# Dealing every PSUM bank by hand instead of by pools, in a fused attention and gated-MLP kernel on one core

The chip is one Trainium2; the kernel runs on one of its cores. The metric is device time in microseconds (us) from launch to end. The profile's span, from the first to the last instruction, is some 1.7 us shorter.

## The reference

```python
x = A_x                                              # 1 x 2048 x 512, bf16
g = sigmoid((x * gate_w).sum(-1, keepdims=True))
# A: linear attention, 32 heads of 16
q, k, v = split(x @ wqkv)
phi_q = concat(softmax(q @ w_phi), softmax(-(q @ w_phi)))     # phi_k likewise
a = (phi_q @ (phi_k.T @ v)) / (phi_q . sum(phi_k) + 1e-6) @ wo
# B: gated MLP with a spatial product over the 2048 rows
z1, z2 = split(gelu(x @ w_in))                       # 688 columns each
b = (z1 * (w_sp @ layernorm(z2) + b_sp)) @ w_out
return g * a + (1 - g) * b
```

## The kernel before

A tile is 128 rows, so there are 16 of them. TensorE runs three stages. First come z2 and z1 of every tile (to about 46 us), then k, v and the accumulation of kv mixed with the first spatial tiles (to about 120 us). Last comes a loop that does, for each tile, one q projection, one spatial half (`gg`), one attention tile (`at`) and one output tile (`acc`). Before an output tile, DMA transposes bring the attention tile's result o and the spatial tile's result `ucat` into place as oT and uT. TensorE's results go to PSUM, of which the program uses eight banks; a bank is free again once ScalarE or VectorE has copied it out, which is called its eviction. Pools give the banks out: a pool hands the next tile a bank that its own plan, made while the kernel is built, sees free first. Below, "old hand-off" is the closing of the one pool and the opening of two others at the start of the last stage, "new hand-off" what the change puts in its place.

```python
def x_T(i):                       # transposes of x tile i, and their copies to SBUF
    parts = [(0, 1), (1, NDT)] if i == 0 else [(0, 2), (2, NDT)] if i == 1 else [(0, NDT)]
    for k, (d0, d1) in enumerate(parts):
        tp = psF.tile([P, NDT, P], BF16, name="tp", tag="pq", bufs=2)
        ...                       # k == 1: copied by ScalarE, else by VectorE

def gate_T():                     # the gate becomes column FH of w_z2, for the second column half
    gt = psF.tile([P, NDT], FP32, name="gt", tag="pq", bufs=2)
    nc.tensor.matmul(gt[:, :], lhsT=gaterow[:, :], rhs=ident[:, 0:NDT], start=True, stop=True)
    nc.vector.tensor_copy(out=w_z2[:, :, FH], in_=gt[:, :])

def ba_store(acc, tt, c0, c1, on_dve):
    ob = work.tile([P, c1 - c0], BF16, name=f"ob{c1 - c0}")       # work: two buffers
    ...
        nc.scalar.activation(out=ob[:, :], in_=acc, func=AF.Copy, scale=g_inv[:, tt:tt + 1])
        nc.scalar.dma_start(out=dst, in_=ob[:, :])

    # the last stage; the k, v stage had psK with six banks for everything
    w_main, w_rem, wo_t = load_out_weights()      # 1.9 MB on ScalarE's queue, issued at once
    psK_cm.__exit__(None, None, None)
    mm_pool = ...tile_pool(name="psG", bufs=2, ...)               # q and spatial tiles
    psC = ...tile_pool(name="psC", bufs=4, ...)                   # output tiles
    attn_tile(0)
    for i in range(NT - 1):
        if i + nq < NT:
            q_tile(i + nq)
        gg_next()
        attn_tile(i + 1)
        if i > 0:
            ba_step(i - 1)        # four outputs make a group; its evictions come together
```

The softmax here doesn't subtract the row's maximum and nothing guards it: scores larger than these inputs give would overflow.

Of the kernel before, what the change touches and what calls it, by code (L numbers as in the profile page):

```python
# [14 lines left out]
P = 128  # L15
# [20 lines left out]
def kernel(  # L36
# [90 lines left out]
    load_z2w(nc.sync, 2)  # L127
    nc.scalar.dma_start(out=gaterow[0:NDT, :], in_=gate_w.rearrange("(dt p) -> dt p", p=P))
    load_z2w(nc.scalar, 3)
    for i in range(2, 4):  # L130
        nc.sync.dma_start(out=xs[:, i, :], in_=x2[i * P:(i + 1) * P, :])
    for h in range(2):
        nc.sync.dma_start(
            out=w_z1[:, 2 * h:2 * h + 2, :], in_=w_in_v[:, 2 * h:2 * h + 2, 0:FH])
# [42 lines left out]
    for i, u in enumerate(ucat):  # L177
        nc.gpsimd.memset(u[:, FH:FPAD] if i % 2 == 0 else u[:, 0:FPAD - FH], 0.0)

    psA_cm = tc.tile_pool(name="psA", bufs=3, space=bass.MemoryType.PSUM, reuse_waits="tile")  # L180
    psA = psA_cm.__enter__()

    def zp_tile():
        return psA.tile([P, 2, CH], FP32, name="zp")

    def z_one(zp, tt, wt, w, dt, j):
        n = HF if j == 0 else w - HF
# [23 lines left out]

    def z2_first_two():
        zps = [zp_tile() for _ in range(2)]

        def one(tt, dt, j):
            z_one(zps[tt], tt, w_z2, FH + 1, dt, j)

        x_T(0)
        warm_up(3, P)
        one(0, 0, 0)  # L220
        x_T(1)
        one(0, 1, 0)
        warm_up(2, P)
        one(1, 0, 0)
        one(1, 1, 0)
        gate_T()
        one(0, 2, 0)
        one(1, 2, 0)
        for dt in range(2):
            one(0, dt, 1)  # L230
            one(1, dt, 1)
        x_T(2)
        one(0, 3, 0)
        one(1, 3, 0)
        one(0, 2, 1)
        one(0, 3, 1)
        z2_out(0, zps[0])
        x_T(3)
        one(1, 2, 1)
        one(1, 3, 1)  # L240
        z2_out(1, zps[1])

    def z1_tile(tt):
        zp = z_mm(tt, w_z1, FH)
# [15 lines left out]
                op0=ALU.subtract, op1=ALU.mult,  # L260
            )

    wp = zp_tile()

    def warm_up(n, w=CH):
        for _ in range(n):
            nc.tensor.matmul(  # L267
                wp[:, 0, 0:w], lhsT=nc.const_aps.tensor(1.0, [P, P], BF16),
                rhs=nc.const_aps.tensor(1.0, [P, w], BF16), start=True, stop=True)

    def x_T(i):
        parts = [(0, 1), (1, NDT)] if i == 0 else [(0, 2), (2, NDT)] if i == 1 else [(0, NDT)]
        for k, (d0, d1) in enumerate(parts):
            tp = psF.tile([P, NDT, P], BF16, name="tp", tag="pq", bufs=2)
            for dt in range(d0, d1):
                nc.tensor.transpose(tp[:, dt, :], xs[:, i, dt * P:(dt + 1) * P], ident[:, :])  # L276
            dst = xT[:, d0:d1, i * P:(i + 1) * P]
            if k == 1:
                nc.scalar.copy(out=dst, in_=tp[:, d0:d1, :])
            else:  # L280
                with tc.high_priority():
                    nc.vector.tensor_copy(out=dst, in_=tp[:, d0:d1, :])

    def gate_T():
        gt = psF.tile([P, NDT], FP32, name="gt", tag="pq", bufs=2)
        nc.tensor.matmul(gt[:, :], lhsT=gaterow[:, :], rhs=ident[:, 0:NDT], start=True, stop=True)
        nc.vector.tensor_copy(out=w_z2[:, :, FH], in_=gt[:, :])

    def b_T():
        bt = psF.tile([P, NT], FP32, name="bt", tag="pq", bufs=2)  # L290
        nc.tensor.matmul(bt[:, :], lhsT=brow[:, :], rhs=ident[:, 0:NT], start=True, stop=True)
        nc.vector.tensor_copy(out=bT[:, :], in_=bt[:, :])

    def wphi_fold():
        wps = psF.tile([P, NDT, P], FP32, name="wps", tag="pq", bufs=2)
        for kc in range(NDT):
            nc.tensor.matmul(
                wps[:, kc, :], lhsT=eexp[:, :],
                rhs=wphiE[:, kc * 8:(kc + 1) * 8, :].rearrange("e h f -> e (h f)"),
                start=True, stop=True,  # L300
            )
        nc.vector.tensor_tensor(
            out=wphi[:, :, :], in0=wps[:, :, :],
            in1=mask_bd[:, None, :].to_broadcast([P, NDT, P]), op=ALU.mult,
        )

    def fold(qk, dt):
        dst = wq_p if qk == 0 else wk_p
        fps = psF.tile([P, CH], FP32, name="fps", tag="pq", bufs=2)
        for kc in range(NDT):  # L310
            nc.tensor.matmul(  # L311
                fps[:, kc * P:(kc + 1) * P],
                lhsT=wqkT[:, qk * 4 + kc, dt * P:(dt + 1) * P],
                rhs=wphi[:, kc, :],
                start=True, stop=True,
            )
        if dt % 2 == 1:
            nc.scalar.copy(out=dst[:, dt, :], in_=fps[:, :])
        else:
            nc.vector.tensor_copy(out=dst[:, dt, :], in_=fps[:, :])  # L320

    with tc.manual_schedule(engines={mybir.EngineType.PE, mybir.EngineType.Activation}):
        warm_up(6)
        warm_up(4, P)
        z2_first_two()
        z2_tile(2)
        z2_tile(3)
        b_T()
        for c in range(NCH):
            ts = list(range(c * 4, c * 4 + 4))  # L330
            for tt in ts:
                if c > 0:
                    z2_tile(tt)
                if c >= 2 and tt % 2 == 0:
                    fold(3 - c, (tt % 4) // 2)
            for tt in ts:
                z1_tile(tt)
                if c >= 2 and tt % 2 == 0:
                    fold(3 - c, 2 + (tt % 4) // 2)
            z2_norm(ts)  # L340
            if c == 1:
                wphi_fold()
# [3 lines left out]
    early_cm.__exit__(None, None, None)  # L346
    psM = ctx.enter_context(
        tc.tile_pool(name="psM", bufs=1, space=bass.MemoryType.PSUM, reuse_waits="tile"))
    psK_cm = tc.tile_pool(name="psK", bufs=6, space=bass.MemoryType.PSUM, reuse_waits="tile")
    mm_pool = psK_cm.__enter__()  # L350
    work = ctx.enter_context(tc.tile_pool(name="work", bufs=2, reuse_waits="tile"))
    kvp_cm = tc.tile_pool(name="kvp", bufs=2, side="right", reuse_waits="tile")
    kvp = kvp_cm.__enter__()

    def mm_tile():
        return mm_pool.tile([P, CH], FP32, name="mm")

    def expo(pool, name, bufs, tt, w):
        ps = mm_tile()
        for dt in range(NDT):  # L360
            nc.tensor.matmul(ps[:, :], lhsT=xT[:, dt, tt * P:(tt + 1) * P], rhs=w[:, dt, :],  # L361
                             start=(dt == 0), stop=(dt == NDT - 1))
        e = pool.tile([P, H, 2, DH], BF16, name=name, bufs=bufs)
        for a in range(2):
            nc.scalar.activation(  # L365
                out=e[:, :, a, :], in_=ps[:, :].rearrange("p (h f) -> p h f", f=DH),
                func=AF.Exp, scale=1.0 - 2.0 * a)
        z = work.tile([P, H, 2], FP32, name="zs")
        nc.vector.tensor_reduce(  # L369
            out=z[:].rearrange("p h a -> p (h a)"), in_=e[:].rearrange("p h a f -> p (h a) f"),  # L370
            axis=AX.X, op=ALU.add,
        )
        return e, z
# [6 lines left out]
            in1=ratio[:, :, None].to_broadcast([P, H, DH]), op=ALU.mult)  # L380

    def k_tile(tt):
        ek, z = expo(kvp, "ek", 5, tt, wk_p)
        rk = kvp.tile([P, H, 2], FP32, name="rk", bufs=3)
        nc.vector.reciprocal(out=rk[:], in_=z[:])
        even_out(ek, z, rk[:, :, 1])
        return ek, rk

    def q_tile(tt):
        eq, z = expo(work, "eq", 3, tt, wq_p)  # L390
        rq = work.tile([P, H], FP32, name="rq")
        nc.vector.reciprocal(out=rq[:], in_=z[:, :, 1])
        even_out(eq, z, rq[:])
        eqT = work.tile([P, 8, P], BF16, name="eqT", bufs=7)
        nc.sync.dma_start_transpose(out=eqT[:, :, :], in_=eq[:].rearrange("p h a f -> p (h a f)"))
        eqTs[tt] = eqT
# [49 lines left out]
        nc.scalar.dma_start(out=w_rem[P - REM:P, :], in_=B_w_out[0:REM, :])  # L446
        return w_main, w_rem, wo_t

    def gg_half(tt, j):
        gp = mm_tile()  # L450
        c0 = (tt % 2) * (FPAD - FH)
        for st in range(NT):
            nc.tensor.matmul(  # L453
# [53 lines left out]
            nc.scalar.dma_start(out=dst, in_=ob[:, :])  # L507

    def acc_tile():
        return psC.tile([P, CH], FP32, name="acc")  # L510

    def ba_tile(tt, cuts=(0, D)):
        for h, (c0, c1) in enumerate(zip(cuts, cuts[1:])):
# [20 lines left out]
    Q_AT = (5, 7, 9, 11, 13, 15)  # L534
    ggs = [(tt, j) for tt in range(NT) for j in range(2)]

    def gg_next():
        tt, j = ggs.pop(0)
        gg_half(tt, j)
        if j == 1:  # L540
            uTs[tt] = u_T(tt)

    with tc.manual_schedule(engines={mybir.EngineType.PE, mybir.EngineType.Activation}):
# [3 lines left out]
        for tt in range(NT):  # L547
# [3 lines left out]
            pend.append((tt, ek, v_tile(tt, rk)))  # L551
            if len(pend) == 3:
                kv_acc(*pend.pop(0))
            gg_next()
            if tt in Q_AT:
                q_tile(Q_AT.index(tt))
        nc.scalar.activation(out=g_el[:, :], in_=glog[:, :], func=AF.Exp)
        nc.vector.tensor_scalar(out=g_1p[:, :], in0=g_el[:, :], scalar1=1.0, scalar2=None, op0=ALU.add)
        nc.vector.reciprocal(out=g_inv[:, :], in_=g_1p[:, :])
        for p_ in pend:  # L560
# [3 lines left out]
        kvw_cm.__exit__(None, None, None)  # L564
        outw = ctx.enter_context(
            tc.tile_pool(name="outw", bufs=1, side="right", reuse_waits="tile"))
        gg_next()
        w_main, w_rem, wo_t = load_out_weights()
        nq = len(Q_AT)
        psK_cm.__exit__(None, None, None)  # L570
        mm_pool = ctx.enter_context(
            tc.tile_pool(name="psG", bufs=2, space=bass.MemoryType.PSUM, reuse_waits="tile"))
        psC = ctx.enter_context(
            tc.tile_pool(name="psC", bufs=4, space=bass.MemoryType.PSUM, reuse_waits="tile"))
        attn_tile(0)
        for i in range(NT - 1):
            if i + nq < NT:
                q_tile(i + nq)
            gg_next()
            attn_tile(i + 1)  # L580
            if i > 0:
                ba_step(i - 1)
# [32 lines left out]
```

## Time and profile before

| | |
|---|---|
| time, median of 3 | 210.49 us (210.31 to 210.69) |
| span of the profiled execution | 208.8 us |
| TensorE | 203.5 us busy, 97% |
| waits of TensorE on another engine or a DMA | q on ucat, twice, 1.0 us in all; transposes on a copy, 0.4 us |

TensorE is the bound, so time is won or lost only where it stands still. The list of waits counts from the modelled end of a matmul and therefore understates a wait. The distances between starts of matmuls do not. Line numbers differ between the kernels: q is L361 before and L369 after, the spatial tile L453 and L460, its eviction (`ucat`) L458 and L465, the exponentials of q L365 and L373.

### The profile page before, as it was taken

The numbers are of one execution on the slowest core, as the hardware profiler recorded it, in microseconds if no ns is written. First come the engines' busy times: TensorE is split into PE (matmuls) and PEld (weight loads), VectorE is DVE, ScalarE is ACT, GpSimd is POOL, SyncE is SP. The second block draws the span as 40 slices with busy tenths as digits, with TensorE's granted clock in tenths as the row PEclk, the third lists the DMA queues.
The fourth block names the chain that finished last, engine by engine and source line by source line (L and its number), as shares of the span: only waits on it lengthen the run. The fifth ranks groups of instructions, "written<-read, shape, count | busy, mean of one in ns | idle before, by whom it ended". The sixth has DMA issues, their size and how long they took to land.

```text
span 208.8 us, 3779 instructions
## 1 busy us (share of the span) xinstructions
PE 203.5 (97%) x1455; PEld 122.2 (59%) x1455; DVE 132.0 (63%) x282; ACT 75.4 (36%) x122; POOL 46.5 (22%) x78
## 2 busy tenths in 40 slices
PE   8999999999999999999999989999999999999994
PEld 4666676665566555656565655555455555565642
DVE  2477786865977776979797676755538563353330
ACT  3666666666322233332323032222251223301322
POOL 7020202020532315334242430422204220010000
PEclk9999999999999999999999999999999999999999
DMA  6998999999932012240422299493562659355542
GB/s 196 230 174 154 250 285 211 290 259 219 290 76 42 0 38 52 41 84 16 81 48 40 50 227 305 84 146 73 105 164 54 115 101 143 75 101 78 129 111 75
DMA packets 88986, 27.20 MB, mean 130 GB/s; under 512 B 82984, under 2 KB 88968, under 8 KB 88968
## 3 DMA queue, kind: packets, MB, share of 16 engines
q1 hardware_dynamic: 84224, 22.43, 56.7%
q10 hardware_dynamic: 4712, 4.53, 7.3%
q8 instruction: 11, 0.18, 0.4%
q14 instruction: 7, 0.06, 0.1%
q0 software_dynamic: 32, 0.00, 0.0%
HBM read 4.41 MB, written 2.10 MB: 31 GB/s over the span
## 4 chain that ended last, share of the span: by engine, by line
PE 93%; ACT 2%; DVE 2%; DMA 1%; ACTq 0%; issue 0%
PE mm L453 34%; PE zp L188 18%; PE mm L361 13%; PE acc L492 8%; PE mm L401 7%; PE acc L490 6%; PE kvacc L417 2%; PE zp L267 2%; PE at L466 2%; DMA out_dram<-ob 1%; PE acc L495 1%; ACT ob L506 1%; PE fps L311 1%; ACT eq L365 1%; PE tp L276 1%; DVE zs L369 1%
## 5 line engine op out<-in xcount | busy, mean ns | idle before, releaser
L453 PE MATMUL mm<-z2all,wspT 128*128 128x344 bf16 x512 | 79.9, 309 | 0.1
L453 PEld LDWEIGHTS <-wspT 128*128 128x128 bf16 x512 | 49.0, 98 | 26.0 <-issue 0.9
L188 PE MATMUL zp<-w_z,xT 128*128 128x344 bf16 (+1 forms) x256 | 40.1, 310 | 0.0
L365 ACT ACTIVATE eq<-mm 128x512 bf16<-128x512 f32 x32 | 17.4, 594 | 51.7 <-PE mm L361 31.0
L369 DVE TENSOR_REDUCE zs<-eq 128x64 f32<-128x1024 bf16 x16 | 19.5, 1219 | 21.7 <-ACT eq L365 21.6
L458 DVE SCALAR_TENSOR_TENSOR ucat<-mm,bT,z1all 128x344 bf16<-128x344 f32 x32 | 17.6, 550 | 21.6 <-PE mm L453 21.6
L188 PEld LDWEIGHTS <-xT 128*128 128x128 bf16 x256 | 24.5, 98 | 11.1 <-issue 0.2
L378 POOL TENSOR_TENSOR eq<-eq,ratio 128x512 bf16<-128x512 bf16 x16 | 16.9, 1058 | 51.1 <-DVE ratio L377 40.2
L365 ACT ACTIVATE ek<-mm 128x512 bf16<-128x512 f32 x32 | 17.3, 600 | 27.1 <-PE mm L361 27.1
L506 ACT ACTIVATE ob<-acc,g_inv 128x512 bf16<-128x512 f32 (+1 forms) x16 | 10.9, 680 | 33.9 <-PE acc L495 23.4
L369 DVE TENSOR_REDUCE zs<-ek 128x64 f32<-128x1024 bf16 x16 | 19.3, 1208 | 2.8 <-ACT ek L365 2.8
L361 PEld LDWEIGHTS <-xT 128*128 128x128 bf16 x128 | 12.4, 98 | 13.9 <-issue 1.2
L492 PE MATMUL acc<-slabs,uT 128*128 128x512 bf16 (+2 forms) x85 | 20.1, 366 | 0.0
L378 POOL TENSOR_TENSOR ek<-ek,ratio 128x512 bf16<-128x512 bf16 x16 | 16.9, 1059 | 2.0 <-DVE ratio L377 1.2
L361 PE MATMUL mm<-wq_p,xT 128*128 128x512 bf16 x64 | 16.4, 379 | 1.0 <-DVE ucat L458 1.0
L490 PE MATMUL acc<-slabs,oT 128*128 128x512 bf16 (+2 forms) x68 | 16.6, 366 | 0.0
L401 PE MATMUL mm<-wv_sb,xT 128*128 128x512 bf16 x64 | 16.4, 379 | 0.0
L361 PE MATMUL mm<-wk_p,xT 128*128 128x512 bf16 x64 | 16.3, 379 | 0.0
L206 DVE BATCH_NORM_STATS2 bn<-z2all 128x6 f32<-128x344 bf16 x32 | 14.9, 503 | 0.0
L245 ACT ACTIVATE z1all<-zp 128x688 bf16<-128x688 f32 x16 | 11.9, 744 | 6.7 <-PE zp L188 6.7
L203 ACT ACTIVATE z2all<-zp 128x688 bf16<-128x688 f32 x16 | 11.8, 744 | 6.8 <-PE zp L188 6.3
L405 POOL CAST vr<-rk 128x32 bf16<-128x32 f32 x16 | 3.4, 212 | 45.7 <-PE mm L453 35.5
(77 smaller groups left out, 155.4 us busy)
## 6 DMA issues: line engine op xcount, KB each, us to landing
out_dram<-ob ACTq DMA_DIRECT2D x15, 128.0 KB, 2.2
slabs<-in_B_w_out_dram ACTq DMA_DIRECT2D x2, 640.0 KB, 6.2
w_z<-in_B_w_in_dram SPq DMA_DIRECT2D x2, 344.0 KB, 5.0
w_z<-in_B_w_in_dram ACTq DMA_DIRECT2D x3, 172.0 KB, 3.4
xs<-in_A_x_dram SPq DMA_DIRECT2D x4, 128.0 KB, 3.2
wv_sb<-in_A_wqkv_dram SPq DMA_DIRECT2D x1, 512.0 KB, 4.6
slabs<-in_A_wo_dram ACTq DMA_DIRECT2D x1, 512.0 KB
uT<-ucat SPq DMA_TRANSPOSE x16, 2.8
```

Of the source, the lines that this page charges most:

```text
L188: nc.tensor.matmul(zp[:, j, 0:n], lhsT=xT[:, dt, tt * P:(tt + 1) * P], rhs=wt[:, dt, j * HF:j * HF + n], start=(dt == 0), stop=(dt == NDT ...
L206: nc.vector.bn_stats(out=bn6[:, tt, j, :], in_=z2v[:, j, :])
L361: nc.tensor.matmul(ps[:, :], lhsT=xT[:, dt, tt * P:(tt + 1) * P], rhs=w[:, dt, :], start=(dt == 0), stop=(dt == NDT - 1))
L365: nc.scalar.activation(out=e[:, :, a, :], in_=ps[:, :].rearrange("p (h f) -> p h f", f=DH), func=AF.Exp, scale=1.0 - 2.0 * a)
L369: nc.vector.tensor_reduce(out=z[:].rearrange("p h a -> p (h a)"), in_=e[:].rearrange("p h a f -> p (h a) f"), axis=AX.X, op=ALU.add,)
L378: nc.gpsimd.tensor_tensor(out=e[:, :, 1, :], in0=e[:, :, 1, :], in1=ratio[:, :, None].to_broadcast([P, H, DH]), op=ALU.mult)
L401: nc.tensor.matmul(v_ps[:, :], lhsT=xT[:, dt, tt * P:(tt + 1) * P], rhs=wv_sb[:, dt, :], start=(dt == 0), stop=(dt == NDT - 1))
L453: nc.tensor.matmul(gp[:, 0:HF], lhsT=wspT[:, st, tt * P:(tt + 1) * P], rhs=z2all[:, st, j * HF:(j + 1) * HF], start=(st == 0), stop=(st == ...
L458: nc.vector.scalar_tensor_tensor(out=ucat[tt % NU][:, c0 + j * HF:c0 + (j + 1) * HF], in0=gp[:, 0:HF], scalar=bT[:, tt:tt + 1], in1=z1all[ ...
L490: nc.tensor.matmul(acc, lhsT=oT[:, g, :], rhs=wo_t[:, g, c0:c1], start=(g == 0), stop=False)
L492: nc.tensor.matmul(acc, lhsT=uT[:, i + ft, :], rhs=w_main[i][:, ft, c0:c1], start=False, stop=False)
L506: nc.scalar.activation(out=ob[:, :], in_=acc, func=AF.Copy, scale=g_inv[:, tt:tt + 1])
```

## The change

It is meant to take away TensorE's three waits. Each half of x tile 1 is to get its own bank, the six banks of the k, v stage are to go on in the last stage in order of age, and one load is to replace two.

```diff
-    for i in range(2, 4):
-        nc.sync.dma_start(out=xs[:, i, :], in_=x2[i * P:(i + 1) * P, :])
+    nc.sync.dma_start(
+        out=xs[:, 2:4, :], in_=x2[2 * P:4 * P, :].rearrange("(i p) d -> p i d", p=P))
 ... # in z2_first_two:
+        tp1 = psA.tile([P, 2, 2 * CH], BF16, name="tp1", tag=next_turn("zp", 3))
-        x_T(1)
+        for h in range(2):
+            x_T(1, 2 * h, 2 * h + 2,
+                tp1[:, h, 0:2 * P].rearrange("p (d n) -> p d n", n=P), on_act=h == 1)
 ...
         gate_T()
-        one(0, 2, 0)
-        one(1, 2, 0)
         for dt in range(2):
             one(0, dt, 1)
             one(1, dt, 1)
+        one(0, 2, 0)
+        one(1, 2, 0)
 ... # in the last stage:
-        psK_cm.__exit__(None, None, None)
-        mm_pool = ...psG, bufs=2
-        psC = ...psC, bufs=4
+        q_bank, g_bank, *acc_banks = [next_turn("mm", 6) for _ in range(6)]
 ...
-                q_tile(i + nq)
-            gg_next()
+                q_tile(i + nq, bank_tile(q_bank))
+            gg_next(bank_tile(g_bank))
```

More of the change, by code (lines that the diff above doesn't have):

```diff
@@ L178, with next_turn, pq_tile @@
         nc.gpsimd.memset(u[:, FH:FPAD] if i % 2 == 0 else u[:, 0:FPAD - FH], 0.0)
-    psA_cm = tc.tile_pool(name="psA", bufs=3, space=bass.MemoryType.PSUM, reuse_waits="tile")
+    psA_cm = tc.tile_pool(name="psA", bufs=1, space=bass.MemoryType.PSUM, reuse_waits="tile")
     psA = psA_cm.__enter__()
+    turn = {"zp": 0, "pq": 0, "mm": 4}
+    def next_turn(kind, n):
+        turn[kind] += 1
+        return f"{kind}{(turn[kind] - 1) % n}"
     def zp_tile():
-        return psA.tile([P, 2, CH], FP32, name="zp")
+        return psA.tile([P, 2, CH], FP32, name="zp", tag=next_turn("zp", 3))
+    def pq_tile(shape, dtype=FP32):
+        return psF.tile(shape, dtype, name="pq", tag=next_turn("pq", 2))
     def z_one(zp, tt, wt, w, dt, j):
@@ L213, in z2_first_two, with warm_up @@
         zps = [zp_tile() for _ in range(2)]
+        tp1 = psA.tile([P, 2, 2 * CH], BF16, name="tp1", tag=next_turn("zp", 3))
+        turn["zp"] -= 1
+        def warm_up(n, w=CH):
+            for _ in range(n):
+                nc.tensor.matmul(
+                    zps[0][:, 1, 0:w], lhsT=nc.const_aps.tensor(1.0, [P, P], BF16),
+                    rhs=nc.const_aps.tensor(1.0, [P, w], BF16), start=True, stop=True)
         def one(tt, dt, j):
             z_one(zps[tt], tt, w_z2, FH + 1, dt, j)
-        x_T(0)
+        warm_up(6)
+        warm_up(5, P)
+        x_T(0, 0, 1, pq_tile([P, 1, P], BF16)[:, :, :])
+        x_T(0, 1, NDT, pq_tile([P, 3, P], BF16)[:, :, :], on_act=True)
         warm_up(3, P)
         one(0, 0, 0)
-        x_T(1)
+        for h in range(2):
+            x_T(1, 2 * h, 2 * h + 2,
+                tp1[:, h, 0:2 * P].rearrange("p (d n) -> p d n", n=P), on_act=h == 1)
         one(0, 1, 0)
@@ L231, in z2_first_two @@
             one(1, dt, 1)
-        x_T(2)
+        one(0, 2, 0)
+        one(1, 2, 0)
+        one(0, 2, 1)
+        one(1, 2, 1)
+        x_T(2, 0, NDT, pq_tile([P, NDT, P], BF16)[:, :, :])
         one(0, 3, 0)
-        one(1, 3, 0)
-        one(0, 2, 1)
         one(0, 3, 1)
         z2_out(0, zps[0])
-        x_T(3)
-        one(1, 2, 1)
+        one(1, 3, 0)
         one(1, 3, 1)
         z2_out(1, zps[1])
+        x_T(3, 0, NDT, pq_tile([P, NDT, P], BF16)[:, :, :])
     def z1_tile(tt):
@@ L261, in z2_norm, with x_T @@
             )
-    wp = zp_tile()
-    def warm_up(n, w=CH):
-        for _ in range(n):
-            nc.tensor.matmul(
-                wp[:, 0, 0:w], lhsT=nc.const_aps.tensor(1.0, [P, P], BF16),
-                rhs=nc.const_aps.tensor(1.0, [P, w], BF16), start=True, stop=True)
-    def x_T(i):
-        parts = [(0, 1), (1, NDT)] if i == 0 else [(0, 2), (2, NDT)] if i == 1 else [(0, NDT)]
-        for k, (d0, d1) in enumerate(parts):
-            tp = psF.tile([P, NDT, P], BF16, name="tp", tag="pq", bufs=2)
-            for dt in range(d0, d1):
-                nc.tensor.transpose(tp[:, dt, :], xs[:, i, dt * P:(dt + 1) * P], ident[:, :])
-            dst = xT[:, d0:d1, i * P:(i + 1) * P]
-            if k == 1:
-                nc.scalar.copy(out=dst, in_=tp[:, d0:d1, :])
-            else:
-                with tc.high_priority():
-                    nc.vector.tensor_copy(out=dst, in_=tp[:, d0:d1, :])
+    def x_T(i, d0, d1, tp, on_act=False):
+        for dt in range(d0, d1):
+            nc.tensor.transpose(tp[:, dt - d0, :], xs[:, i, dt * P:(dt + 1) * P], ident[:, :])
+        dst = xT[:, d0:d1, i * P:(i + 1) * P]
+        if on_act:
+            nc.scalar.copy(out=dst, in_=tp)
+        else:
+            with tc.high_priority():
+                nc.vector.tensor_copy(out=dst, in_=tp)
     def gate_T():
-        gt = psF.tile([P, NDT], FP32, name="gt", tag="pq", bufs=2)
+        gt = pq_tile([P, NDT])
         nc.tensor.matmul(gt[:, :], lhsT=gaterow[:, :], rhs=ident[:, 0:NDT], start=True, stop=True)
@@ L289, in b_T @@
     def b_T():
-        bt = psF.tile([P, NT], FP32, name="bt", tag="pq", bufs=2)
+        bt = pq_tile([P, NT])
         nc.tensor.matmul(bt[:, :], lhsT=brow[:, :], rhs=ident[:, 0:NT], start=True, stop=True)
@@ L294, in wphi_fold @@
     def wphi_fold():
-        wps = psF.tile([P, NDT, P], FP32, name="wps", tag="pq", bufs=2)
+        wps = pq_tile([P, NDT, P])
         for kc in range(NDT):
@@ L308, in fold @@
         dst = wq_p if qk == 0 else wk_p
-        fps = psF.tile([P, CH], FP32, name="fps", tag="pq", bufs=2)
+        fps = pq_tile([P, CH])
         for kc in range(NDT):
@@ L322 @@
     with tc.manual_schedule(engines={mybir.EngineType.PE, mybir.EngineType.Activation}):
-        warm_up(6)
-        warm_up(4, P)
         z2_first_two()
@@ L348 @@
         tc.tile_pool(name="psM", bufs=1, space=bass.MemoryType.PSUM, reuse_waits="tile"))
-    psK_cm = tc.tile_pool(name="psK", bufs=6, space=bass.MemoryType.PSUM, reuse_waits="tile")
-    mm_pool = psK_cm.__enter__()
     work = ctx.enter_context(tc.tile_pool(name="work", bufs=2, reuse_waits="tile"))
@@ L353, with bank_tile, expo @@
     kvp = kvp_cm.__enter__()
+    def bank_tile(tag):
+        return psM.tile([P, CH], FP32, name="mm", tag=tag)
     def mm_tile():
-        return mm_pool.tile([P, CH], FP32, name="mm")
-    def expo(pool, name, bufs, tt, w):
-        ps = mm_tile()
+        return bank_tile(next_turn("mm", 6))
+    def expo(pool, name, bufs, tt, w, ps):
         for dt in range(NDT):
@@ L382, in k_tile @@
     def k_tile(tt):
-        ek, z = expo(kvp, "ek", 5, tt, wk_p)
+        ek, z = expo(kvp, "ek", 5, tt, wk_p, mm_tile())
         rk = kvp.tile([P, H, 2], FP32, name="rk", bufs=3)
@@ L387, in k_tile, with q_tile @@
         return ek, rk
-    def q_tile(tt):
-        eq, z = expo(work, "eq", 3, tt, wq_p)
+    def q_tile(tt, ps):
+        eq, z = expo(work, "eq", 3, tt, wq_p, ps)
         rq = work.tile([P, H], FP32, name="rq")
@@ L447, in load_out_weights, with gg_half @@
         return w_main, w_rem, wo_t
-    def gg_half(tt, j):
-        gp = mm_tile()
+    def gg_half(tt, j, gp):
         c0 = (tt % 2) * (FPAD - FH)
@@ L509, in acc_tile @@
     def acc_tile():
-        return psC.tile([P, CH], FP32, name="acc")
+        acc_banks.append(acc_banks.pop(0))
+        return bank_tile(acc_banks[-1])
     def ba_tile(tt, cuts=(0, D)):
@@ L535, with gg_next @@
     ggs = [(tt, j) for tt in range(NT) for j in range(2)]
-    def gg_next():
+    def gg_next(gp):
         tt, j = ggs.pop(0)
-        gg_half(tt, j)
+        gg_half(tt, j, gp)
         if j == 1:
@@ L553 @@
                 kv_acc(*pend.pop(0))
-            gg_next()
+            gg_next(mm_tile())
             if tt in Q_AT:
-                q_tile(Q_AT.index(tt))
+                q_tile(Q_AT.index(tt), mm_tile())
         nc.scalar.activation(out=g_el[:, :], in_=glog[:, :], func=AF.Exp)
@@ L566 @@
             tc.tile_pool(name="outw", bufs=1, side="right", reuse_waits="tile"))
-        gg_next()
+        gg_next(mm_tile())
         w_main, w_rem, wo_t = load_out_weights()
         nq = len(Q_AT)
-        psK_cm.__exit__(None, None, None)
-        mm_pool = ctx.enter_context(
-            tc.tile_pool(name="psG", bufs=2, space=bass.MemoryType.PSUM, reuse_waits="tile"))
-        psC = ctx.enter_context(
-            tc.tile_pool(name="psC", bufs=4, space=bass.MemoryType.PSUM, reuse_waits="tile"))
+        q_bank, g_bank, *acc_banks = [next_turn("mm", 6) for _ in range(6)]
         attn_tile(0)
@@ L577 @@
             if i + nq < NT:
-                q_tile(i + nq)
-            gg_next()
+                q_tile(i + nq, bank_tile(q_bank))
+            gg_next(bank_tile(g_bank))
             attn_tile(i + 1)
```

## The prediction

> **What bounds the kernel now.** I read the page's busy shares first, then the chain that ended last, then the waits by pair, and last the timeline around every place where TensorE's next matmul starts later than the one before it needs.
>
> ```profile
> PE 203.5 (97%) x1455; PEld 122.2 (59%) x1455; DVE 132.0 (63%) x282; ACT 75.4 (36%) x122; POOL 46.5 (22%) x78
> ...
> PE 93%; ACT 2%; DVE 2%; DMA 1%; ACTq 0%; issue 0%
> ```
>
> TensorE is busy 97% of 208.8 us and is 93% of the chain; the granted clock is 9 tenths or more in every slice. So the change is worth what it moves in TensorE's waits, nothing else. In the list of waits, TensorE itself waits in two pairs only:
>
> ```profile
> PE mm L361 <- DVE ucat L458: 1.0, 2, 0.5
> ...
> PE tp L276 <- DVE xT L282: 0.4, 1, 0.4
> ```
>
> Modelled ends hide part of a wait, so I take the distance from the start of one matmul to the start of the next. The two waits of L361 (the q projection) in the timeline:
>
> ```profile
> 122.46 0.42 PE L466 MATMUL at<-kvz,eqT 128*128 128x68 bf16 x8
> ...
> 122.80 0.58 DVE L458 SCALAR_TENSOR_TENSOR ucat<-mm,bT,z1all 128x344 bf16<-128x344 f32 x1
> ...
> 123.42 1.02 PE L361 MATMUL mm<-wq_p,xT 128*128 128x512 bf16 x4 [0.55 <-DVE ucat L458]
> ...
> 126.82 0.58 DVE L458 SCALAR_TENSOR_TENSOR ucat<-mm,bT,z1all 128x344 bf16<-128x344 f32 x1 [2.40 <-PE mm L453]
> ...
> 127.45 1.02 PE L361 MATMUL mm<-wq_p,xT 128*128 128x512 bf16 x4 [0.41 <-DVE ucat L458]
> ```
>
> The q tile stands still until the eviction (ucat) of the spatial tile just before it frees the bank. Eight attention matmuls at 0.032 us apart end their slots at 122.72 and 126.87, so the waits are 0.70 and 0.58 us.
>
> **What the skill says.** "PSUM — Partial Sum Buffer", section "PSUM bank collisions raise a hardware error": TensorE may not write a bank while ScalarE or VectorE reads it, so semaphores guard banks, not addresses. The trace agrees in kind: q starts 0.04 us after the eviction ends. The same page, "Engine vs sequencer instructions", calls the ScalarE and VectorE queues strict first in, first out. The trace agrees: at 182.33 below an eviction whose data had been ready since 179.9 runs only after a reduction that stood ahead of it. "TensorE: Matmul & The Clock Gate", section "Wait — 56ns, not 53.3ns?": 106.7 and 426.7 ns per matmul of 128 and 512 columns cold, 55.6 and 215.7 warm. The trace has 0.107 and 0.427 us up to about 5.9 us, and 0.056 and 0.216 us after.
>
> **The change part by part.** All arithmetic and tile counts stay; TensorE gets one more warm-up matmul. I compared the built programs for what each bank wait waits on, and put the times of the old trace beside them. D is the new kernel's lag behind the old.
>
> 1. Start. One more cold warm-up, 0.107 us; x's first tile had landed at 3.70 us, just before its transposes start at 3.79, so it delays them. The clock goes full at about 5.9 us whatever the kernel does, and work that slides past it runs at double rate: about 0.05 us stays. D = +0.05.
>
> 2. The transposes of x tile 1.
>
> ```profile
> 5.27 0.29 DVE L282 COPY xT<-tp 128x256 bf16<-128x256 bf16 x1 [0.92 <-PE tp L276]
> 5.62 0.37 PE L276 MATMUL tp<-ident,xs 128*128 128x128 bf16 x2 [0.38 <-DVE xT L282]
> ```
>
> The intent is to end this wait with a bank for each half. But both halves are slices of one tile, and the built program still has the second half's first transpose wait on the first half's copy. Gain 0, where the intent has 0.59 us (4.93 + 0.107 to 5.62).
>
> 3. The gate column. The copy of the transposed gate into w_z2 is waited for by the first matmul of the second column half.
>
> ```profile
> 6.62 0.18 DVE L287 CAST w_z<-gt 128x4 bf16<-128x4 f32 x1 [1.06 <-PE gt L286]
> ...
> 6.86 0.39 PEld L188 LDWEIGHTS <-xT 128*128 128x128 bf16 x3 [0.17 <-issue]
> ```
>
> Before, two matmuls of 0.145 us stood between and filled 0.29 of that time. The change moves them behind. The copy is not earlier, so those 0.29 us are idle: D = +0.34. The merged load cannot repay it: the third slice of w_z2 landed at 5.91, x tile 2 at 6.45, and TensorE asked at 6.44 and 7.44. x tile 3 (7.14) was used at 8.25. All those loads are hidden.
>
> 4. Rest of the first stage and the k, v stage. The z banks rotate as before over three pairs with the same releasers. The first k tile now takes the bank of the last weight fold, whose ScalarE eviction ended at 45.88, while the first k matmul started at 45.84: with 0.05 us for the semaphore a wait of 0.09. D = +0.43. From 46 to 120 us no bank wait of the old kernel shows, and the new rotation has the same six banks at the same distance, so nothing is to be won.
>
> 5. The two q waits go: the six banks pass on in order of age, and q and the spatial tile get a bank each. -0.70 and -0.58. But the first output tile then asks sooner for oT, whose transpose was issued at 125.43 and landed at 130.19 (the weights for the output were loading); it was used at 130.87. That is 0.68 us of slack, and the landing moves with D = +0.43 as it hangs on the kv accumulation. So of 1.28 us only 0.68 survives: D = 0.43 - 0.68 = -0.25.
>
> 6. After the first group of four outputs.
>
> ```profile
> 153.94 0.69 ACT L506 ACTIVATE ob<-acc,g_inv 128x512 bf16<-128x512 f32 x1 [0.51 <-DMA out_dram<-ob]
> ...
> 155.06 1.03 PE L361 MATMUL mm<-wq_p,xT 128*128 128x512 bf16 x4
> 155.10 2.17 ACT L365 ACTIVATE eq<-mm 128x512 bf16<-128x512 f32 x4 [0.47 <-ACT ob L506]
> ...
> 156.23 2.49 PE L453 MATMUL mm<-z2all,wspT 128*128 128x344 bf16 x16
> ```
>
> ScalarE evicts four outputs, waiting for stores, and reaches the previous q tile's two exponentials only at 155.10; they end at 156.19. The old pool gave this q tile the other bank, so q ran at 155.06 and only the spatial tile waited, 0.31 us. In the new kernel q has one bank for good: it waits to 156.23, and its four matmuls (4 x 0.216 = 0.86) come after. +0.86: D = +0.61.
>
> 7. After the second group, with no q tiles left.
>
> ```profile
> 180.51 1.22 DVE L369 TENSOR_REDUCE zs<-eq 128x64 f32<-128x1024 bf16 x1 [3.29 <-ACT eq L365]
> ...
> 182.11 2.50 PE L453 MATMUL mm<-z2all,wspT 128*128 128x344 bf16 x16
> ...
> 182.33 0.57 DVE L458 SCALAR_TENSOR_TENSOR ucat<-mm,bT,z1all 128x344 bf16<-128x344 f32 x1
> ```
>
> The spatial tiles alternated over two banks; now they have one, and q's lies unused. The tile at 182.11 must wait for the eviction that VectorE ends at 182.90: 0.79 + 0.05 = +0.84. D = +1.45.
>
> From there to the end every bank's last reader is over 1 us ahead, and the last 4.6 us hang on the same transposes. Sum: 0.05 + 0.29 + 0.09 - 0.68 + 0.86 + 0.84 = +1.45 us on 210.49, some 211.9.
>
> **The rivals.**
> - The intent comes true: three waits gone (0.59 + 0.70 + 0.58 = 1.87 us) and no new one: 208.6. For it: TensorE is the bound, and these are its only listed waits. Against: the remaining wait in the built program, the landing of oT, and parts 6 and 7, which the list of waits of the old kernel cannot show because its pool dodged them.
> - Losses without the gain: the landing of oT slips further and part 5 gives nothing: D = +2.13, 212.6. For it: the queue was saturated there and the landing took 4.8 us instead of the median 2.9.
> - The late waits are smaller, because ScalarE's outputs hang on stores that landed 2 to 4 us after their issue. If stores land 0.5 us sooner in both places, D is about +0.5: 211.0.
> - The merged load reorders the start: 128 KB more ahead of w_z2's last slice could push it from 6.21 past its use. It is used at about 8.3 in the new order, so I give this little.
>
> **Range and chances.** I take 211.8, a little below the sum as most of its terms are upper sides of waits. 210.9 to 212.6 holds the third rival and the failed gain. Two per cent is 4.2 us, over twice any sum here, so within 2% gets 0.98 and each side 0.01.
>
> **What would show it.** In the list of waits: the wait of the transposes on the copy of xT stays near 0.4; the pair q on ucat is gone; new are q on the exponentials of q, over 1 us, and the spatial tile on ucat, near 0.8; the first output tile waits on oT near 130. In the timeline a hole after the gate matmul of about 0.4. It would be wrong if the program's waits ended earlier than the old trace's times suggest, above all at the places of parts 6 and 7: if TensorE shows no stop near 155 and 182, the time is near 209.5 to 210.5.

## The result

The changed kernel took 212.7 us (median of four runs, 211.54 to 212.89) beside 210.4 us for the kernel before. The ratio is 1.010, with an interval from 1.006 to 1.014: within 2%, and about 2 us slower. Here and below a ratio is the mean time of one kernel's fast runs over the mean of the other's fast runs of the same rounds, so it is not quite the ratio of the medians. Microseconds of gain below are a difference of two such ratios times 210.4.

The page of the changed kernel, busy times and chain (18 of its 1456 matmuls left no record, so its busy time is a little low):

```profile
PE 202.3 (96%) x1438; PEld 121.6 (58%) x1456; DVE 131.4 (62%) x282; ACT 75.4 (36%) x122; POOL 46.5 (22%) x78
...
PE 86%; DMA 6%; ACT 3%; DVE 1%; issue 1%; ACTq 1%; DVEq 0%
```

TensorE fell from 93% to 86% of the chain: other engines and DMAs now hold it up. The list of TensorE's waits names them (line, engine waited for, total, times, longest):

```profile
PE mm L497 <- DMA oT<-o: 1.7, 1, 1.7
PE mm L369 <- ACT eq L373: 1.0, 1, 1.0
...
PE mm L460 <- DVE ucat L465: 0.6, 1, 0.6
PE tp L286 <- DVE xT L292: 0.4, 1, 0.4
PE zp L196 <- DVE w_z L297: 0.3, 1, 0.3
```

The pair q on ucat is gone, as meant. The transposes' wait, which was to go as well, has stayed. Four new waits stand beside it: the first output tile on oT, q on its own exponentials, the spatial tile on ucat, and the second column half on the gate's column.

The hole behind the gate matmul, in the timeline of the changed kernel:

```profile
6.12 0.17 PE L296 MATMUL pq<-ident,gaterow 128*128 128x4 bf16 x1
6.35 0.17 DVE L297 CAST w_z<-pq 128x4 bf16<-128x4 f32 x1 [0.95 <-PE pq L296]
6.58 0.60 PE L196 MATMUL zp<-w_z,xT 128*128 128x345 bf16 x3 [0.29 <-DVE w_z L297]
```

TensorE has nothing to do from the gate matmul at 6.12 to the copy's end, and goes on at 6.58. And the start of the first output tile, with the issue of the transposing DMA that it waits for:

```profile
125.79 1.35 SPq L486 DMA_TRANSPOSE oT<-o  x1
...
131.61 1.04 PE L497 MATMUL mm<-slabs,oT 128*128 128x512 bf16 x4 [1.74 <-DMA oT<-o]
```

oT landed at 131.57, 5.8 us after its issue, and TensorE had been ready since 129.7.

Between two traces I follow D, the start of the same matmul after minus before. The second look is the first experiment below.

| behind which place | D predicted | D, first look | D, second look |
|---|---|---|---|
| the first two z tiles | +0.34 | +0.02 | +0.32 |
| first k tile | +0.43 | +0.10 | +0.41 |
| first q wait (the q tile now starts early) | -0.27 | -0.61 | -0.31 |
| second q wait | -0.85 | -1.19 | -0.88 |
| first output tile | -0.25 | +0.72 | +0.41 |
| after the first group of outputs | +0.61 | +1.58 | +1.25 |
| after the second group, and the end | +1.45 | +2.32 | +2.00 |

(The two middle predictions are its -0.70 and -0.58 taken one after the other.) The steps agree within 0.1 us but for two: the start, which the first look shows 0.3 us better, and the wait for oT, which is 1.3 to 1.9 us where the prediction's own numbers left 0.6.

### The profile page after: what moved, and what is told of

It reads as the page before. It is cut to its first block, busy times and chain, and to the rows that moved or that the text cites. A ratio compares the mean times of both kernels' runs of the same rounds, so it can differ in the third digit from the quotient of the medians.

```text
span 211.2 us, 3762 instructions
## 1 busy us (share of the span) xinstructions
PE 202.3 (96%) x1438; PEld 121.6 (58%) x1456; DVE 131.4 (62%) x282; ACT 75.4 (36%) x122; POOL 46.5 (22%) x78
## 4 chain that ended last, share of the span: by engine, by line
PE 86%; DMA 6%; ACT 3%; DVE 1%; issue 1%; ACTq 1%; DVEq 0%
PE mm L460 31%; PE zp L196 18%; PE mm L369 12%; PE mm L499 7%; PE mm L409 7%; PE mm L497 5%; DMA out_dram<-ob 3%; DMA oT<-o 3%; ACT ob L513 2%; PE kvacc L425 2%; PE zp L227 2%; PE at L473 1%; ACT eq L373 1%; PE mm L502 1%; PE pq L321 1%
## 5 line engine op out<-in xcount | busy, mean ns | idle before, releaser
L513 ACT ACTIVATE ob<-mm,g_inv 128x512 bf16<-128x512 f32 (+1 forms) x16 | 10.9, 680 | 34.6 <-PE mm L502 24.0
L499 PE MATMUL mm<-slabs,uT 128*128 128x512 bf16 (+2 forms) x85 | 20.1, 366 | 0.0
L497 PE MATMUL mm<-slabs,oT 128*128 128x512 bf16 (+2 forms) x62 | 15.8, 365 | 2.1 <-DMA oT<-o 1.7
L499 PEld LDWEIGHTS <-uT 128*128 128x128 bf16 x85 | 8.1, 98 | 9.2
## 6 DMA issues: line engine op xcount, KB each, us to landing
out_dram<-ob ACTq DMA_DIRECT2D x15, 128.0 KB, 1.9
xs<-in_A_x_dram SPq DMA_DIRECT2D x2, 128.0 KB, 3.3
```

What stands on the lines that cost most here:

```text
L497: nc.tensor.matmul(acc, lhsT=oT[:, g, :], rhs=wo_t[:, g, c0:c1], start=(g == 0), stop=False)
L499: nc.tensor.matmul(acc, lhsT=uT[:, i + ft, :], rhs=w_main[i][:, ft, c0:c1], start=False, stop=False)
```

## The experiments

My theory was the prediction's, with the oT step open. The rivals: oT was one execution's bad luck; the late stops come from the backlog of ScalarE and VectorE and would only move; the start is neutral. The experiments ran in four sets, the first to the fourth, the fifth to the eighth, the ninth to the eleventh and the twelfth; each set on one chip with its own runs of the kernel before.

**1. The changed kernel once more**, no edit.

> The changed kernel, unaltered, a second look. Theory A (the oT transposes queue behind the output weights in every execution, because the new order leaves less work ahead of them): the first output tile again waits 1.5 to 2.0 us on oT, and the kernel is 2.0 to 2.6 us behind the kernel before. Theory B (the 1.9 us were one execution's luck with the queues): the wait is 0.6 to 1.1 us and the lag 1.2 to 1.7 us. For the start, both: if the clock's switch to full speed is a matter of phase, the lag at the end of the first two tiles is anywhere from 0 to 0.35 us; if the change moves it, it is 0.0 again.

212.57 us, ratio 1.0097 (1.0075 to 1.0119). The list has oT at 1.1 us (1.29 us between starts), and the lag is 2.0 us: neither theory cleanly. The wait comes back in all six traces of the new hand-off that load the weights at once, but between starts it is 0.98 to 1.29 us in five of them, so 1.9 us was high. The start lags 0.32 us, so the first look's +0.02 was not the change's doing. The distances between starts of equal matmuls show when TensorE's clock goes full (107 ns for 128 columns before, 56 after): from about 3.7 us in the first look, about 5.8 here, and between 5.8 and 6.0 in the kernel before.

**2. Let the two banks trade places.**

```diff
+            if i == 6 or i > 10:
+                q_bank, g_bank = g_bank, q_bank
             if i + nq < NT:
                 q_tile(i + nq, bank_tile(q_bank))
```

> The changed kernel, but in the last stage q and the spatial tile trade their two banks before the seventh round (right after the first four outputs), and the spatial tiles alternate over both banks once no q is left. My theory (parts 6 and 7: one bank each for good makes q wait for the exponentials near 156 and the spatial tile for ucat near 183): both waits vanish, 0.85 + 0.74 = 1.6 us less than the changed kernel, an end about 0.8 us behind the kernel before. Rival (the two stops come from ScalarE's and VectorE's backlog itself and only move): less than 0.5 us gained, the stops show up at the next tile.

210.79 us, ratio 1.0014 (0.9992 to 1.0037): 1.7 us won, 1.6 expected. Both stops left the list of waits; only 0.2 us of a spatial tile's wait on the exponentials stayed at 156. The rival, that the stops merely move, falls. The second stop in the second look:

```profile
183.49 0.57 DVE L465 SCALAR_TENSOR_TENSOR ucat<-mm,bT,z1all 128x344 bf16<-128x344 f32 x1
...
184.11 1.18 PE L460 MATMUL mm<-z2all,wspT 128*128 128x344 bf16 x7 [0.58 <-DVE ucat L465]
```

and both places with the swap, without the waits:

```profile
155.72 1.03 PE L369 MATMUL mm<-wq_p,xT 128*128 128x512 bf16 x4
...
182.82 1.48 PE L460 MATMUL mm<-z2all,wspT 128*128 128x344 bf16 x9
```

**3. Half of `w_out` a round later** (0.75 MB of the 1.9 MB of output weights), behind the second q tile of the last stage.

```diff
-        for i in range(2):
-            nc.scalar.dma_start(out=w_main[i], ...)
-        nc.scalar.dma_start(out=w_rem[0:REM, :], ...)
-        nc.scalar.dma_start(out=w_rem[P - REM:P, :], ...)
+        load_main(0)              # and in the loop, behind attn_tile(i + 1):
+            if i == 1:
+                load_late()       # w_main[1] and both parts of w_rem
```

> The changed kernel with half of the output weights (the second main slab of 5 x 128 x 512 and the two remainders, about 0.8 MB) issued one round later, behind the second q tile of the last stage. My theory (the transposes of uT and oT stand behind the weight loads): oT of the first tile lands before 129.5 us and the wait of the first output matmul on oT falls from 1.9 to under 0.3 us, the total 1.4 to 1.9 us less. Rival (oT is late because the transposes stand behind each other or behind o itself): the wait stays over 1.0 us and the total within 0.5 us. A third outcome: the second output tile now waits for its late slab, up to 1 us, at 134 to 136 us.

oT landed at 128.54 us, 3.1 us after its issue in place of 5.4, and is waited for no more. The first output tile in the second look and here:

```profile
131.30 1.04 PE L497 MATMUL mm<-slabs,oT 128*128 128x512 bf16 x4 [1.12 <-DMA oT<-o]
```

```profile
129.65 1.02 PE L503 MATMUL mm<-slabs,oT 128*128 128x512 bf16 x4
```

It came 1.65 us sooner, but 0.37 of that is this trace's quicker start (D is -0.05 behind the first two z tiles, in the second look +0.32). The time is 211.41 us, ratio 1.0049 (1.0032 to 1.0067): 1.0 us won, less than I had expected. At the stop near 183, 0.3 us were given back (D less that of the second look goes from -1.65 to -1.38 there); without the start's 0.37 that is the 1.0 us of the ratios. The late weights are not waited for.

Why it works shows in the DMA view of the second look, for 123.5 to 128.0 us (queue, packets, MB, share; then what was issued in that window, with the time from issue to landing):

```profile
q10 hardware_dynamic: 1529, 1.53, 107.3%
...
eqT<-eq SPq DMA_TRANSPOSE x1, 6.3
oT<-o SPq DMA_TRANSPOSE x1, 5.4
uT<-ucat SPq DMA_TRANSPOSE x1, 4.7
```

q10, ScalarE's queue of plain loads, is the only one with packets. Three transposes were issued on SyncE's queue in that window, and not one of their packets moved before the last slab was nearly in. In all ten traces that load the weights at once, oT landed 1.0 to 1.3 us behind the last of them.

**4. The gate's wait filled again.**

```diff
         gate_T()
+        one(0, 2, 0)
+        one(1, 2, 0)
         for dt in range(2):
             one(0, dt, 1)
             one(1, dt, 1)
-        one(0, 2, 0)
-        one(1, 2, 0)
```

> The changed kernel with the two matmuls of the third slice moved back to right behind the gate matmul, as in the kernel before. My theory (part 3: they filled the wait for the gate column): the wait of the z matmul on w_z, 0.3 us in the list, is gone, and the first two tiles end 0.2 to 0.3 us sooner where the clock is full there; total 0.2 to 0.3 us less, which may drown in the run-to-run spread. Rival (slices land too late for them there): the same 0.3 us are then waited for the load, total unchanged.

The wait on w_z left the list, and behind the first two tiles the kernel is 0.33 us ahead of the second look. 0.04 of that came before the gate matmul (6.38 for 6.42), as the clock went full a little sooner; the other 0.29 is the hole. So the mechanism holds. The total does not show it: ratio 1.0093 (1.0060 to 1.0127), as two of six runs took 213.2 and 213.7 us. The time is inconclusive, the trace is not.

**5. Two tiles for the two halves of x tile 1.**

```diff
-        zps = [zp_tile() for _ in range(2)]
-        tp1 = psA.tile([P, 2, 2 * CH], BF16, name="tp1", tag=next_turn("zp", 3))
-        turn["zp"] -= 1
+        zps = [zp_tile()]
+        tp_a = psA.tile([P, 2, 2 * CH], BF16, name="tp_a", tag="zp1")
+        tp_b = psA.tile([P, 2, 2 * CH], BF16, name="tp_b", tag="zp2")
 ...
+        zps.append(zp_tile())     # behind the transposes
```

> The changed kernel with the two halves of x tile 1 transposed into two separate tiles in two pairs of banks, as the change's words say. My theory (part 2: the copy is waited for only because both halves are slices of one tile): the pair tp on xT leaves the list of waits, the second half's first transpose starts 0.11 us after the first half's last instead of 0.69, and the first two tiles end 0.3 to 0.6 us sooner than in the second look at the changed kernel if the clock goes full at the same time; total 0.3 to 0.6 us less. Rival (the next thing behind is as late: the copy of x tile 0 or the second slice of w_z2): a new wait of 0.3 us or more there, total less than 0.2 us down.

The timeline, and two lines of the chain in the stretch from 6 to 8 us:

```profile
4.48 0.28 PE L287 MATMUL tp_a<-ident,xs 128*128 128x128 bf16 x2
4.59 0.27 PE L287 MATMUL tp_b<-ident,xs 128*128 128x128 bf16 x2
```

```profile
2.20 5.05 DMA xs<-in_A_x_dram
...
7.29 0.40 PE pq L287 x4
```

The second half follows the first without a gap. So it was the shared tile, not the bank, that made it wait. But TensorE now arrives early at x tile 2 (also because its clock was full from 3.7 us in this trace) and waits there for the merged load, which landed at 7.25. From the last matmul's start (6.90) to the first transpose (7.29) it is 0.39 us where one matmul takes 0.146, so 0.25 us are lost. As a load of its own, in the kernel before, tile 2 had landed at 6.45. The total won is 0.3 us by the ratios (1.0082, 1.0063 to 1.0102), within the noise of either outcome. My theory and the rival are both partly right.

**6. Only the one load**, in the kernel before. The diff is the first hunk of the change.

> The kernel before with x tiles 2 and 3 in one load, nothing else of the change. All theories that I hold: no effect, within 0.2 us of the kernel before, as both loads land over 0.8 us ahead of their use. Against that stands the rival of the merged load: the last slice of w_z2 lands 0.3 us or more later and the first two tiles end later. It also serves as one more look at the old hand-off: if the landing of the first oT is a matter of luck with the queues, it lands anywhere from 130.0 to 131.2 here; if it hangs on the issue times, within 0.2 us of 130.2 and TensorE does not wait for it.

210.54 us, ratio 1.0007 (0.9987 to 1.0026): no effect, as expected. oT landed at 130.80 here, and its slack was 0.23 us in place of 0.71, although the last stage is that of the kernel before.

**7. The late weights in the kernel before.**

> The kernel before with half of the output weights issued one round later, as in the third experiment. If the late weights help only where TensorE comes early enough to wait for oT (my theory: in the kernel before oT had 0.7 us of slack): no gain, within 0.3 us of the kernel before. Rival (the weight loads slow the kernel before as well, by other ways): 0.5 us or more gained.

209.66 us, ratio 0.9975 (0.9955 to 0.9996): 0.5 us won, which I had not expected. But the reason is not the rival's. The second of the two q tiles no longer waits for ucat:

```profile
126.58 1.02 PE L361 MATMUL mm<-wq_p,xT 128*128 128x512 bf16 x4
```

In the kernel before this line carried a wait of 0.41 us. In the built program the pool had dealt the two banks differently: q keeps the bank of the first q tile until the first group of outputs, where q and the spatial tiles trade banks, as they do there in the kernel before. The load's new place shifted the pool's plan, so this run changes two things at once. Its trace tells them apart: D is -0.30 from the start on, -0.87 at that q tile, and still -0.87 at the first output tile. The 0.57 us of the bank are the whole gain, and the late loads brought nothing more, as my theory had it. The run also shows that what a pool deals hangs on edits far away.

**8. Four buffers for the evicted outputs** in the changed kernel.

```diff
-        ob = work.tile([P, c1 - c0], BF16, name=f"ob{c1 - c0}")
+        ob = outw.tile([P, c1 - c0], BF16, name=f"ob{c1 - c0}", bufs=4 if c1 - c0 == D else 2)
```

> The changed kernel with four instead of two buffers for the evicted outputs; the order of instructions on every engine is the same. My theory: the stops at 156 and 183 us come of two things together, the single banks and ScalarE standing 1.4 us for the store of the first output before it may evict the third, and so reaching the exponentials of q too late. Then the exponentials start 1.3 to 1.4 us sooner, both stops vanish, and the gain is 0.85 + 0.74 = 1.6 us, as much as the bank swap gave. Rival (the in-order work of ScalarE alone makes them late): exponentials less than 0.5 us sooner and under 0.6 us gained.

The timeline of the second look around the first group of outputs, with two buffers:

```profile
153.17 0.69 ACT L513 ACTIVATE ob<-mm,g_inv 128x512 bf16<-128x512 f32 x1 [1.39 <-DMA out_dram<-ob]
...
155.49 1.09 ACT L373 ACTIVATE eq<-mm 128x512 bf16<-128x512 f32 x2 [0.47 <-ACT ob L513]
...
156.62 1.02 PE L369 MATMUL mm<-wq_p,xT 128*128 128x512 bf16 x4 [0.98 <-ACT eq L373]
```

and with four:

```profile
151.46 0.69 ACT L513 ACTIVATE ob<-mm,g_inv 128x512 bf16<-128x512 f32 x1 [0.45 <-ACT ob L513]
...
153.72 1.08 ACT L373 ACTIVATE eq<-mm 128x512 bf16<-128x512 f32 x2 [0.47 <-ACT ob L513]
...
154.85 1.02 PE L369 MATMUL mm<-wq_p,xT 128*128 128x512 bf16 x4
```

ScalarE stood 1.39 us before its third eviction, until the store of the first had given its buffer back. With four buffers it stands 0.45 us, no more than before the second. From the first eviction to the exponentials it takes 4.55 us (149.17 to 153.72) in place of 5.53 (149.96 to 155.49): 0.98 us sooner, less than the 1.3 that I had written. It is enough: both stops are gone from the list of waits. 210.78 us, ratio 1.0015 (0.9991 to 1.0038), 1.7 us won, the same as by the bank swap.

So each of the two stops needs two things at once, a bank that only one kind of tile may use and a ScalarE held up by a store. Taking away either cures them.

**9. Bank swap and late weights together**, the start as changed.

> The changed kernel with the two banks trading places and the late half of the weights, the start as changed. My theory: both q waits stay gone (1.3 us), oT is not waited for, the stops at 156 and 183 are gone, and only the start's 0.3 us are lost: 0.9 us under the kernel before, about 209.5. Rival (the saved time comes back at the next landing, that of the second oT or the late slab): at or above the kernel before.

209.72 us, ratio 0.9967 (0.9946 to 0.9988): 0.7 us under the kernel before. Of all waits only the two at the start are left on the list.

**10. All five edits together.**

> The changed kernel with all five edits together: the two banks trade places, half of the output weights a round later, the gate's wait filled, two tiles for the halves of x tile 1, four output buffers. If the lags are separate waits on one bound engine, they add up: from 212.6 us take 1.8 (banks or output buffers, which cure the same stops once), 1.2 (late weights), 0.3 (gate) and 0.3 to 0.5 (two tiles), that is 208.8 to 209.0, 1.4 us under the kernel before. Rival (something behind them takes over, such as the late slab or the landing of x tile 2, which stood in the way in the run with two tiles): over 209.6.

208.93 us, ratio 0.9931 (0.9908 to 0.9955). The parts added up, and this version beats both kernels: 1.5 us under the kernel before. Its list of TensorE's waits holds the program's entry and nothing else:

```profile
PE zp L227 <- PEq L614: 0.8, 1, 0.8
```

The list leaves out what the distances between starts show. In this trace, whose clock was full from 4.0 us, 0.28 us are lost behind the gate matmul (5.58 to 5.89; the third slice of w_z2 landed at 5.85) and 0.17 before x tile 2 (6.91 to 7.22; it landed at 7.18). The rival of the fourth experiment, a slice that lands too late, is thus real once TensorE is early.

**11. The start of the change alone**, with the old pools from the k, v stage on.

> The start of the change alone (transposes, gate order, one load, fixed rotation of the banks in the first stage), with the pools of the kernel before from the k, v stage on. My theory: 0.25 to 0.35 us behind the kernel before, all of it before 9 us, spread by when the clock goes full; the waits of q on ucat are back at 0.5 each and no other is new. Rival (the start is neutral and only its clock differs by chance): within 0.1 us.

211.08 us, ratio 1.0022 (1.0000 to 1.0045): some 0.5 us, with an interval that holds my 0.25 to 0.35 and also nothing. In the trace D is +0.36 behind the first two tiles, and the q waits are back at 0.5 each. One such D decides nothing, as the next part shows. A further +0.19 comes at 156, where the spatial tile waits 0.3 for the exponentials; the sixth run has the same wait and +0.17 there. In both, ScalarE stood about 1.6 us for the first store (1.58 and 1.60) where the two traces of the kernel before have 1.38 and 1.41. The sixth run has only the one load of this start, so I put it down to the scatter of the stores; two traces on each side do not prove it.

**12. The kernel before once more**, one look.

> The kernel before, unaltered, a second look. The prediction gave oT 0.68 us of slack from one trace, where it landed 9.41 us after the first load of the output weights was issued. If that trace was a lucky one (theory), oT lands here 9.5 to 9.9 us after that issue, and the first output matmul has 0.2 to 0.5 us of slack, as the old hand-off showed in the two other runs that have it (9.89 and 9.61 us). Rival (the hand-dealt banks slow the loads and the old order does not): 9.4 us again, within 0.1.

oT landed 9.70 us after the first weight load's issue (counted from the end of the issuing instruction, here and below), and the first output tile had 0.42 us of slack. So the first trace of the kernel before was the luckiest of four.

## Why the prediction was right or wrong

That the change stays within 2% was right, and so was the sign. The time, 211.8, was 0.9 us short of the median of 212.7, which lies 0.1 above the range.

- *Step 1 and step 3, the start.* The gate's hole was right: filling it brought the 0.29 us that stood there. That the second look has +0.32 where +0.34 stood for the whole start is luck: over the seven traces with the start as changed, D runs from -0.19 to +0.60 (mean 0.22), and over the three of the start of before from -0.30 to 0 (mean -0.15). The means lie 0.37 apart, near the prediction, so the rival of a neutral start is unlikely; single pairs of traces tell nothing. "The clock goes full at about 5.9 us whatever the kernel does" fell: over fourteen traces it went full anywhere between 3.5 and 6.7 us, also in two runs of the same kernel. "TensorE: Matmul & The Clock Gate" of the Trainium skill, section "What's actually happening", gives a reason, which no run here tests: the activity window is free-running and does not start with the kernel. The first look, which had it at 3.7 us, shows a start 0.3 us better than the second.
- *Step 2, the copy's wait.* Right: it stayed at 0.4 in the list, 0.6 to 0.7 us between starts, and separate tiles removed it. In the trace of the fifth experiment the merged load, which I had called hidden, took back 0.25 us of the intent's 0.59. In the two looks at the kernel as changed it was hidden, with 0.5 and 0.1 us to spare.
- *Step 4.* Right: +0.08 and +0.09 in the two looks, +0.09 predicted.
- *Step 5, the q waits and oT.* The gain was right, 0.71 and 0.57 for 0.70 and 0.58. The term that failed is "That is 0.68 us of slack, and the landing moves with D": with it the wait for oT would be 0.60 us, and the wait measured 1.91 and 1.29 in the two looks and 0.98 to 1.26 in four other traces, mean 1.28 of the six. The slack was read from one trace. oT landed 9.41 us after the first weight load's issue in it, but 9.61 to 9.89 in the three other traces with the old hand-off, which leaves 0.23 to 0.51 us of slack. In the six with the new hand-off and the weights at once it was 9.78 to 10.70, mean 10.08. Of the second look's missing 0.69 us, 0.24 is the luck of the first trace (mean of the four, 9.65, less 9.41). For the other 0.43, the difference of the means, the two ranges overlap, and the first look alone makes 0.12 of it; whether the new hand-off itself slows the loads stays open.
- *Steps 6 and 7.* Right in place, cause and size: +0.85 and +0.74 for +0.86 and +0.84. What the steps left out is that the store of the first output is half of the cause; the row at 153.94 in the prediction already shows a wait of ScalarE on it.
- *The rivals.* The one that came true is the second, "Losses without the gain", at 212.6, and for the reason that it named: a queue already full. I gave it the edge of the range only. The first fell with the remaining wait and the new ones, the third with steps 6 and 7 at full size. The fourth was wrong in its place: w_z2's last slice landed at 6.3 to 7.3 us in the traces with the merged load and was not waited for; what can cost time is the landing of x tile 2, once TensorE is early.

Where did the expected gain of 1.9 us go? 0.6 never came, as the two halves share a tile. The other 1.28 came, and TensorE spent it at once in front of oT. The 2 us of loss are the start with the gate's hole, the first k tile's bank and the two single banks.

## What to carry to other kernels

A hand-dealt rotation must be checked against the worst moment of every reader, not against the average: here a bank for each kind of tile was fine in all rounds but two, right behind a group of evictions that waited for stores. Before counting a removed wait as a gain, look for the next landing behind it, and take its slack from several executions, since one trace gave 0.7 us where four gave 0.2 to 0.7. And the dependency goes by tile: slices of one tile in separate banks still wait for each other.

## What the Trainium skill lacked or had wrong

- "DMA: Bandwidth & Descriptors", section "Queues, rings and completion order", says that each DMA engine goes round-robin between the queues for which it has work, one packet at a time. Here it did not look so: from 123.5 to 128.0 us the plain loads' queue moved 1529 packets and the transposes' queue none, with a transpose pending since 124.48 and another since 125.82; they landed 6.3 and 5.4 us after their issue. In the first look that queue was not shut out: 32 packets of it, the last 4-byte ones of the transpose that was issued at 119.59 and landed at 126.92, moved among the plain loads from 124.0 to 126.5, and the loads ran at 304 GB/s there (123.5 to 127.0), in the second look at 338 with none of these. That may be why its oT was the latest of all. No run tells whether the descriptors of the later transposes came late or were passed over, so the page need not be wrong.
- No page that I read says what that means for a kernel: transposes issued behind 1.9 MB of plain loads on the other queue landed 1.0 to 1.3 us after the last of those loads, in ten of ten traces, and holding back 0.75 MB of them brought oT home 3.1 us after its issue in place of 5.4.
- "TensorE: Matmul & The Clock Gate", section "What's actually happening", gives the switch to full clock a scatter of 500 ns either way. Fourteen traces of kernels with nearly the same first 4 us have it between 3.5 and 6.7 us, at least 2.5 us apart (before 3.7 in one, after 6.2 in another), and the two looks at the changed kernel differ by 0.3 us at the start. The free-running window of the same section, about 3.4 us long, would allow a spread of that size.
